# rstd of the first four tiles by ScalarE square root and VectorE reciprocal, bulk loads issued by SyncE, and a reordered prologue

## The chip, the cores and the metric

The kernel runs on 1 core of one Trainium2 chip. Times are device microseconds (us) of one execution; a median of several executions is quoted. Most of the argument is read from traces, where the place of a single instruction is given to 0.01 us. A trace is one execution of each kernel.

Engines in profile lines: PE is TensorE (matmuls), PEld its weight loads, DVE is VectorE, ACT is ScalarE, POOL is GpSimd, SP is SyncE. SPq and ACTq are the queues on which these two issue DMAs.

## The reference, cut to what matters

The input x has 2048 tokens of 448 values. One layer norm feeds two branches, a linear attention with softmax features and a mixer with two MLPs; the output is their sum.

```python
x = A_x
xn = _layernorm(x, axis=-1)          # (x - mean) / sqrt(var + 1e-5)
return x + _A_ref(xn, A_wqkv, A_w_phi, A_wo) + _B_ref(xn, B_w1, B_w2, B_w3, B_w4)
```

Every later step needs xn, and TensorE needs it transposed (features on the partitions).

## The kernel before: the parts that the change and the argument touch

The tokens are 16 tiles of 128. For each tile VectorE takes statistics, GpSimd makes rstd as (var + eps) to the power -0.5, VectorE applies it, TensorE transposes the tile into PSUM, and ScalarE (for tiles 10 and 11 VectorE) copies the transposed tile to xnT in SBUF.

```python
def ln_stats(stt, mvt, src, i):                      # VectorE
    R.ew(dve, "bn_stats", stt[:, i, 0:6], src[:, i, 0:D])
    R.ew(dve, "bn_aggr", mvt[:, i, 0:2], stt[:, i, 0:6])

def ln_scale(mvt, rst, a, n, neg):                   # GpSimd
    R.ew(pool, "tensor_scalar", mvt[:, a:a + n, 2], mvt[:, a:a + n, 1], LN_EPS, 1.0, op0=ALU.add, op1=ALU.mult)
    R.ew(pool, "tensor_tensor", rst[:, a:a + n, 0], mvt[:, a:a + n, 2], mhalf[:, 0:n], op=ALU.pow)
    # [cut]
for i in range(10):
    ln1_stats(i, 1, 0)            # ln_stats, then ln_scale, of tile i
    if i:
        ln1_apply(dve, i - 1)
```

PSUM is used as four pairs of banks, 0 to 3. The program makes two instructions on one pair exclude each other: a matmul that starts a new result waits until the engine that reads the old one is done. The prologue is a list of steps played in order. Each engine keeps the order in which its own instructions were recorded, so the list is also the order of ScalarE's queue. The number after a step such as `(xn_T, 5, 2)` is its PSUM pair; for V, WA and WC it stands in a table.

- `spin`: matmuls without use, which keep TensorE busy while it waits.
- `xn_T, i, b`: transposes of tile i into pair b, then the copy to xnT.
- `V(i, k)`: half k of the value projection of tiles i and i + 1 (8, then 6 matmuls). `v_out` is its copy by ScalarE.
- `WA(g, k)`, `WC(g, k)`: parts of x times w1 for tokens 512 g to 512 g + 511; `wa_out` and `wc_out` are their gelus on ScalarE.
- `FO`: folding w_phi into weights. After the prologue come eight rounds "ps" of k and q projections, then the second MLP in pairs p of w3 columns, halves `a(p)` and `b(p)`, with the up-projection `f` and the attention tiles `N` between.

```python
vps = {i: v_pair(i, b) for i, b in ((0, 2), (2, 3), (4, 3), (6, 1), (8, 1), (10, 1), (14, 3))}
wcs = {g: wc_pair(g, b) for g, b in ((0, 2), (1, 3), (2, 0), (3, 3))}
spin(19, 256)
play([(xn_T, 0, 0), (spin, 3, 256), (xn_T, 1, 1), (spin, 4, 256), V(0, 0), (xn_T, 2, 0), V(0, 1), (xn_T, 3, 1),
      (spin, 2, 256), V(2, 0), (v_out, 0, 2), WA(0, 0), (xn_T, 4, 1), (xn_T, 5, 2), V(2, 1), (v_out, 2, 3),
      WA(0, 1), (xn_t, 6, 1, 0), WC(0, 0), (xn_t, 7, 1, 1), (xn_e, 6, 1, 2), WC(0, 1), (wa_out, 0, 0), (wc_out, 0, 2),
      # [cut: V(4), V(6)]
      WA(1, 0), (xn_T, 8, 2, 2), WC(1, 0), WA(1, 1), (xn_T, 10, 1, 2, "DVE"), (ln1_end,), WC(1, 1), (wc_out, 1, 3),
      (wa_out, 1, 0), V(8, 0), FO(1, 0, 0), V(8, 1), (v_out, 8, 1),
      # [cut]
```

The softmax here doesn't subtract the row's maximum and nothing guards it: scores larger than these inputs give would overflow.

## Time and profile before

Median 176.25 us (176.02 to 176.55, 3 runs).

| what | before | where it is read |
|---|---|---|
| PE busy | 168.9 of 174.0 us, 97% | page, part 1 |
| chain that ended last | PE for 94% | page, part 4 |
| first real transposes / of tile 3 | 5.70 / 9.30 us | timeline |
| V(8,0) starts | 20.70 us | timeline |
| break before V(8,0) | 19.86 to 20.70 us | chain in order of time |
| round ps 0 | 31.52 to 37.21 us | timeline |

These are lines of the page of the kernel before: busy time by engine, and the chain of work that ended last.

```profile
PE 168.9 (97%) x2254; PEld 90.4 (52%) x2254; DVE 114.2 (66%) x258; ACT 81.9 (47%) x94; POOL 92.3 (53%) x131
PE 94%; DVE 3%; issue 1%; POOL 0%; ACT 0%; DVEq 0%
```

TensorE is the limit for nearly all of the span. A change of the prologue can win where TensorE waits, at the start and in the break before V(8,0), and where matmuls are stretched without idle time in the records, as in round ps 0 (see the prediction).

This is the timeline of the kernel before at the start. The columns are start in us, duration in us, engine, line, operation, output<-input and count; in square brackets is the idle time before it and who ended it.

```profile
3.41 0.63 DVE L212 BATCH_NORM_STATS2 st<-xtok 128x6 f32<-128x448 bf16 x1
4.35 0.19 POOL L212 TENSOR_SCALAR mv<-mv 128x1 f32<-128x1 f32 x1 [1.69 <-DVE mv L212]
4.62 0.57 POOL L212 TENSOR_TENSOR rs<-mv,mhalf 128x1 f32<-128x1 f32 x1
5.23 0.41 DVE L212 TENSOR_SCALAR xn<-xtok,mv,rs 128x512 bf16<-128x512 bf16 x1 [0.25 <-POOL rs L212]
6.31 0.38 DVE L212 TENSOR_SCALAR xn<-xtok,mv,rs 128x512 bf16<-128x512 bf16 x1
...
7.41 0.41 DVE L212 TENSOR_SCALAR xn<-xtok,mv,rs 128x512 bf16<-128x512 bf16 x1
...
8.54 0.41 DVE L212 TENSOR_SCALAR xn<-xtok,mv,rs 128x512 bf16<-128x512 bf16 x1
```

The two GpSimd steps of tile 0 take 0.84 us from 4.35 to 5.19, in which VectorE does the statistics of tile 1. Tiles 0 to 3 are applied at 5.23, 6.31, 7.41 and 8.54.

And this is the timeline of the kernel before at the break.

```profile
19.45 0.40 PE L204 MATMUL bank<-ident,xn 64*128 64x64 bf16 x16
19.68 0.49 PE L200 MATMUL bank<-xnT,w 64*128 64x256 bf16 x6
19.88 0.76 DVE L212 COPY xnT<-bank 128x512 bf16<-128x512 bf16 x2 [0.34 <-PE bank L204]
20.70 0.93 PE L200 MATMUL bank<-wv,xnT 64*128 64x448 bf16 x8 [0.53 <-DVE xnT L212]
```

V(8,0), the last line, has its tiles but not its pair: VectorE is still copying tiles 10 and 11 out of it. The idle time in brackets counts from the modelled end of the last matmul; the chain counts 0.84 us from the last issue.

### The profile page before, as it was taken

The numbers are of one execution on the slowest core, as the hardware profiler recorded it, in microseconds if no ns is written. First come the engines' busy times: TensorE is split into PE (matmuls) and PEld (weight loads), VectorE is DVE, ScalarE is ACT, GpSimd is POOL, SyncE is SP. The second block draws the span as 40 slices with busy tenths as digits, with TensorE's granted clock in tenths as the row PEclk, the third lists the DMA queues.
The fourth block names the chain that finished last, engine by engine and source line by source line (L and its number), as shares of the span: only waits on it lengthen the run. The fifth ranks groups of instructions, "written<-read, shape, count | busy, mean of one in ns | idle before, by whom it ended". The sixth has DMA issues, their size and how long they took to land.

```text
span 174.0 us, 5178 instructions
## 1 busy us (share of the span) xinstructions
PE 168.9 (97%) x2254; PEld 90.4 (52%) x2254; DVE 114.2 (66%) x258; ACT 81.9 (47%) x94; POOL 92.3 (53%) x131
## 2 busy tenths in 40 slices
PE   7899899999999999999999999999999999999993
PEld 5466577454555554554544555545545555545451
DVE  4999876185999999985687962445417424474711
ACT  2269866779877777956225322224214222224000
POOL 3786470007779999940549389440721714523740
PEclk9999999999999999999999999999999999999999
DMA  5994532115991102034012732034411220314331
GB/s 159 326 263 79 134 73 50 31 39 148 399 348 41 30 17 47 4 34 90 10 24 60 79 77 59 28 87 95 90 30 53 60 57 4 85 30 34 83 105 30
DMA packets 32678, 15.20 MB, mean 87 GB/s; under 512 B 24080, under 2 KB 32016, under 8 KB 32656
## 3 DMA queue, kind: packets, MB, share of 16 engines
q1 hardware_dynamic: 29888, 12.96, 31.8%
q10 hardware_dynamic: 2768, 1.92, 3.5%
q8 instruction: 17, 0.28, 0.7%
q14 instruction: 5, 0.04, 0.1%
HBM read 7.14 MB, written 1.84 MB: 52 GB/s over the span
## 4 chain that ended last, share of the span: by engine, by line
PE 94%; DVE 3%; issue 1%; POOL 0%; ACT 0%; DVEq 0%
PE bank L200 92%; PE bank L204 1%; DVE vaug L212 1%; DVE st L212 1%; DVE xnT L212 0%; DVE xn L212 0%; ACT xnT L208 0%; POOL rs L212 0%; DVE mv L212 0%; DVEq L173 0%; DVE gT L212 0%; POOL mv L212 0%
## 5 line engine op out<-in xcount | busy, mean ns | idle before, releaser
L208 ACT ACTIVATE phik<-bank 128x1024 bf16<-128x1024 f32 (+1 forms) x44 | 42.3, 984 | 60.2 <-PE bank L200 60.2
L200 PE MATMUL bank<-gT,w 64*128 64x512 bf16 x392 | 50.0, 377 | 0.0
L212 DVE TENSOR_TENSOR vaug<-bank,vaug 128x464 f32<-128x464 f32 (+3 forms) x65 | 32.6, 512 | 23.0 <-PE bank L200 21.4
L200 PE MATMUL bank<-w,phik 64*128 64x448 bf16 (+1 forms) x420 | 45.0, 349 | 0.0
L212 POOL TENSOR_TENSOR xnT<-vaug 128x196 bf16<-128x196 f32 (+1 forms) x32 | 18.1, 587 | 46.3 <-DVE vaug L212 46.3
L200 PEld LDWEIGHTS bank<-w,phik 64*128 64x128 bf16 (+1 forms) x420 | 21.7, 94 | 21.2 <-issue 0.4
L212 POOL TENSOR_TENSOR phik<-phik,rks 128x1792 bf16<-128x1792 bf16 x8 | 25.6, 3214 | 10.6 <-DVE rks L212 10.5
L200 PEld LDWEIGHTS bank<-gT,w 64*128 64x128 bf16 x392 | 17.5, 94 | 17.5 <-ACT phik L208 0.4
L212 POOL TENSOR_TENSOR vaug<-xn,xtok 128x448 f32<-128x448 bf16 x16 | 16.2, 1033 | 0.2 <-DVE vaug L212 0.2
L212 DVE TENSOR_REDUCE ksum<-phik 128x64 f32<-128x1792 bf16 x8 | 16.1, 2010 | 0.0
L212 DVE RECIPROCAL vaug<-bank 128x16 f32<-128x16 f32 x16 | 4.1, 257 | 17.9 <-PE bank L200 17.9
L200 PE MATMUL bank<-xnT,wpq 64*128 64x512 bf16 x112 | 14.7, 376 | 0.0
L200 PE MATMUL bank<-wv,xnT 64*128 64x448 bf16 x112 | 13.5, 351 | 0.6 <-DVE xnT L212 0.5
L212 POOL TENSOR_TENSOR rs<-mv,mhalf 128x1 f32<-128x1 f32 (+2 forms) x20 | 13.0, 651 | 1.7
L200 PE MATMUL bank<-wo,xnT 64*128 64x448 bf16 (+1 forms) x106 | 13.4, 349 | 0.0
L200 PE MATMUL bank<-xnT,w 64*128 64x512 bf16 (+2 forms) x168 | 13.3, 306 | 0.0
L200 PE MATMUL bank<-w,hT 64*128 64x448 bf16 x112 | 13.2, 349 | 0.0
L200 PE MATMUL bank<-wpk,xnT 64*128 64x448 bf16 x112 | 13.2, 349 | 0.0
L212 DVE TENSOR_TENSOR xn<-bank,xn 128x512 bf16<-128x512 f32 (+1 forms) x16 | 9.2, 620 | 3.1 <-PE bank L200 3.1
L212 DVE BATCH_NORM_STATS2 st<-xtok 128x6 f32<-128x448 bf16 x16 | 9.9, 617 | 0.0
L208 ACT ACTIVATE xnT<-bank 128x512 bf16<-128x512 bf16 x12 | 6.7, 595 | 5.7 <-PE bank L204 5.5
L212 POOL TENSOR_SCALAR g_tok<-xn,rs 128x512 bf16<-128x512 bf16 x12 | 9.1, 771 | 0.3
(64 smaller groups left out, 169.4 us busy)
## 6 DMA issues: line engine op xcount, KB each, us to landing
w<-in_B_w_dram SPq DMA_DIRECT2D x2, 896.0 KB, 5.8
out_dram<-vaug SPq DMA_DIRECT2D x15, 112.0 KB, 1.9
w<-in_B_w_dram SPq DMA_DIRECT2D x1, 1568.0 KB, 11.6
xtok<-in_A_x_dram ACTq DMA_DIRECT2D x2, 448.0 KB, 7.6
xtok<-in_A_x_dram SPq DMA_DIRECT2D x2, 224.0 KB, 5.9
w<-in_B_w_dram ACTq DMA_DIRECT2D x2, 224.0 KB, 6.1
wo<-in_A_wo_dram SPq DMA_DIRECT2D x2, 224.0 KB, 6.7
w<-in_B_w_dram SPq DMA_DIRECT2D x1, 336.0 KB, 3.5
```

The source lines that it names most:

```text
L200: self.op("PE", lambda e: e.matmul(out, lhsT, rhs, start=start, stop=stop, skip_group_check=True), [out], [lhsT, rhs], tile=self._tile(lhsT))
L204: self.op("PE", lambda e: e.transpose(out, in_, ident), [out], [in_, ident], tile=self._tile(in_))
L208: self.op("ACT", lambda e: e.activation(out, in_, func, **kw), [out], [in_] + aps)
L212: self.op(eng, lambda e: getattr(e, name)(out, *args, **kw), [out], aps)
```

## The change

Its intent: tiles 0 to 3 should reach TensorE earlier by replacing the GpSimd power with a square root on ScalarE and a reciprocal on VectorE. ScalarE must then be free early, so SyncE issues the bulk loads. Later tiles come a little later, and the order and pairs of the prologue are set to that; tiles 10 and 11 get another pair. Gelu now needs a second table load. Round ps 0 is reordered. The diff, cut to its core:

```diff
+        load_lap(w1, B_w1)                       # all on SyncE, after x tiles 4 to 7
+        load_x(8, 4)
+        load_x(12, 4)
+        R.dma(wphi[0:CR, :, :], ...)
-        R.op("ACT", lambda e: e.preload_act_table_set("gelu_apprx_tanh_and_others"), [], [])
-        load_lap(w1, B_w1, ("ACT", "ACT"))
-        load_x(8, 4, "ACT")
-        load_x(12, 4, "ACT")
-        R.dma(wphi[0:CR, :, :], ..., "ACT")
+        tables("sqrt_and_others")
+        R.ew(dve, "memset", epsb[:, :], LN_EPS)
@@
-        for i in range(10):
+        def ln1_two(i):
+            for j in (i, i + 1):
+                ln_stats(st, mv, xtok, j)
+                R.act(rs[:, j, 1:2], mv[:, j, 1:2], ACT.Sqrt, bias=epsb[:, 0:1])
+            for j in (i, i + 1):
+                R.ew(dve, "reciprocal", rs[:, j, 0:1], rs[:, j, 1:2])
+                ln1_apply(dve, j)
+        ln1_two(0)
+        # [cut: spins and the transposes of tiles 0 and 1, as before]
+        ln1_two(2)
+        for i in range(4, 10):
             ln1_stats(i, 1, 0)
-            if i:
+            if i > 4:
                 ln1_apply(dve, i - 1)
@@
-        vps = {... (2, 3), (4, 3), (6, 1), ...}      # and wcs (1, 3)
+        vps = {... (2, 3), (4, 1), (6, 3), ...}      # and wcs (1, 2)
-              (spin, 2, 256), V(2, 0), (v_out, 0, 2), WA(0, 0), (xn_T, 4, 1), (xn_T, 5, 2), V(2, 1), (v_out, 2, 3),
-              WA(0, 1), (xn_t, 6, 1, 0), WC(0, 0), (xn_t, 7, 1, 1), (xn_e, 6, 1, 2), WC(0, 1), (wa_out, 0, 0), (wc_out, 0, 2),
+              (spin, 2, 256), V(2, 0), (v_out, 0, 2), (tables, "gelu_apprx_tanh_and_others"), WA(0, 0), (xn_T, 4, 1),
+              V(2, 1), (v_out, 2, 3), (xn_T, 5, 2), WA(0, 1), WC(0, 0), (xn_T, 6, 3), WC(0, 1), (wc_out, 0, 2),
@@   # further on
-              WA(1, 0), (xn_T, 8, 2, 2), WC(1, 0), WA(1, 1), (xn_T, 10, 1, 2, "DVE"), ...
+              ..., WC(1, 1), (xn_T, 8, 1, 2), (wc_out, 1, 2), WA(1, 1), (wa_out, 1, 0), (xn_T, 10, 3, 2, "DVE"), ...
@@   # round ps 0
+            if not ps:
+                play([(k[0],), (q[0],), (k[1],), (k_exp, 0, 1, 0), (k_exp, 0, 1, 1), (w[0],), (q[1],), (q_exp, 0, 0, 0),
+                      (q_exp, 0, 0, 1), V(14, 0), (w[1],), (v_out, 12, 2, "DVE"), V(14, 1), (v_out, 14, 3), (k_norm, 0)])
+                continue
```

More of the change, by code (lines that the diff above doesn't have):

```diff
@@ L306, in bass_parallel_sum__linear_kernel_hedgehog__mixer_s_mlp__prompt_kernel @@
         mhalf = new("mhalf", 8, F32)
+        epsb = new("epsb", 8, F32)
         h3T = view(phik_r, 2 * FC * 512).rearrange("p (b c f) -> p b c f", b=2, c=FC)
@@ L360, in bass_parallel_sum__linear_kernel_hedgehog__mixer_s_mlp__prompt_kernel @@
         load_x(6, 2)
+        load_lap(w1, B_w1)
+        load_x(8, 4)
+        load_x(12, 4)
+        R.dma(wphi[0:CR, :, :], A_w_phi.rearrange("(c q) e f -> (q e) c f", q=4))
         def load_wT(t):
@@ L378, in bass_parallel_sum__linear_kernel_hedgehog__mixer_s_mlp__prompt_kernel, with tables @@
         vp = vaug.rearrange("p t (h e) -> p (t h) e", e=HP)
-        R.op("ACT", lambda e: e.preload_act_table_set("gelu_apprx_tanh_and_others"), [], [])
-        load_lap(w1, B_w1, ("ACT", "ACT"))
-        load_x(8, 4, "ACT")
-        load_x(12, 4, "ACT")
-        R.dma(wphi[0:CR, :, :], A_w_phi.rearrange("(c q) e f -> (q e) c f", q=4), "ACT")
+        def tables(name):
+            R.op("ACT", lambda e: e.preload_act_table_set(name), [], [])
+        tables("sqrt_and_others")
         R.ew(pool, "memset", ident[:, :], 0.0)
@@ L778, in play @@
                 f[0](*f[1:])
-        for i in range(10):
+        def ln1_two(i):
[6 more added lines that the diff above has]
+        ln1_two(0)
+        spin(19, 256)
+        play([(xn_T, 0, 0), (spin, 3, 256), (xn_T, 1, 1)])
+        ln1_two(2)
+        for i in range(4, 10):
             ln1_stats(i, 1, 0)
-            if i:
+            if i > 4:
                 ln1_apply(dve, i - 1)
@@ L799, in ln1_end @@
             late_3()
-        vps = {i: v_pair(i, b) for i, b in ((0, 2), (2, 3), (4, 3), (6, 1), (8, 1), (10, 1), (14, 3))}
+        vps = {i: v_pair(i, b) for i, b in ((0, 2), (2, 3), (4, 1), (6, 3), (8, 1), (10, 1), (14, 3))}
         was = {g: wa_pair(g, b) for g, b in ((0, 0), (1, 0), (2, 0), (3, 2))}
-        wcs = {g: wc_pair(g, b) for g, b in ((0, 2), (1, 3), (2, 0), (3, 3))}
+        wcs = {g: wc_pair(g, b) for g, b in ((0, 2), (1, 2), (2, 0), (3, 3))}
         wds = {h: wd_pair(h, b) for h, b in ((0, 1), (1, 0))}
@@ L820, in FO @@
             return (fps[t, m][k],)
-        spin(19, 256)
-        play([(xn_T, 0, 0), (spin, 3, 256), (xn_T, 1, 1), (spin, 4, 256), V(0, 0), (xn_T, 2, 0), V(0, 1), (xn_T, 3, 1),
-              (spin, 2, 256), V(2, 0), (v_out, 0, 2), WA(0, 0), (xn_T, 4, 1), (xn_T, 5, 2), V(2, 1), (v_out, 2, 3),
-              WA(0, 1), (xn_t, 6, 1, 0), WC(0, 0), (xn_t, 7, 1, 1), (xn_e, 6, 1, 2), WC(0, 1), (wa_out, 0, 0), (wc_out, 0, 2),
-              V(4, 0), V(6, 0), V(4, 1), (v_out, 4, 3), V(6, 1), (v_out, 6, 1),
-              WA(1, 0), (xn_T, 8, 2, 2), WC(1, 0), WA(1, 1), (xn_T, 10, 1, 2, "DVE"), (ln1_end,), WC(1, 1), (wc_out, 1, 3),
-              (wa_out, 1, 0), V(8, 0), FO(1, 0, 0), V(8, 1), (v_out, 8, 1),
+        play([(spin, 4, 256), V(0, 0), (xn_T, 2, 0), V(0, 1), (xn_T, 3, 1),
+              (spin, 2, 256), V(2, 0), (v_out, 0, 2), (tables, "gelu_apprx_tanh_and_others"), WA(0, 0), (xn_T, 4, 1),
+              V(2, 1), (v_out, 2, 3), (xn_T, 5, 2), WA(0, 1), WC(0, 0), (xn_T, 6, 3), WC(0, 1), (wc_out, 0, 2),
+              V(4, 0), (xn_T, 7, 3), (wa_out, 0, 0), V(4, 1), (v_out, 4, 1), V(6, 0),
+              WC(1, 0), V(6, 1), (v_out, 6, 3), WA(1, 0), WC(1, 1), (xn_T, 8, 1, 2), (wc_out, 1, 2), WA(1, 1), (wa_out, 1, 0),
+              (xn_T, 10, 3, 2, "DVE"), (ln1_end,), V(8, 0), FO(1, 0, 0), V(8, 1), (v_out, 8, 1),
               WA(2, 0), FO(1, 0, 1), FO(1, 2, 0), WA(2, 1), (wa_out, 2, 0), FO(1, 2, 1),
@@ L860, in bass_parallel_sum__linear_kernel_hedgehog__mixer_s_mlp__prompt_kernel @@
             w[1]()
-            if ps:
-                w2_out(side[ps], 2)
-            else:
-                v_out(12, 2, "DVE")
-                vps[14][0]()
+            w2_out(side[ps], 2)
             q[1]()
@@ L868, in bass_parallel_sum__linear_kernel_hedgehog__mixer_s_mlp__prompt_kernel @@
                 q_exp(2 * ps, 0, s)
-            if not ps:
-                vps[14][1]()
-                v_out(14, 3)
             if ps in (3, 5):
```

## The prediction

> **What bounds the kernel now.** TensorE: the page has PE busy 168.9 of 174.0 us (97%), and the chain of waits is PE for 94%. From the second operand of V(2,0) at 10.27 us to 171.27 the chain has one break: 19.86 to 20.70, where V(8,0) waits for a VectorE copy (2 x 0.38 us) of tiles 10 and 11, because that copy holds the PSUM pair which V(8,0) needs. So the change can only win in the first 10 us, in that break, and in hidden stalls. Round ps 0 (31.52 to 37.21) takes 5.69 us; its 56 matmuls at their steady spacing (about 0.094 us for 448 columns, 0.107 for 512) are about 5.4. At most 0.3 us is there.
>
> **First 10 us (timeline).** Before: bn_stats 0 at 3.41, GpSimd add and pow (0.19 + 0.57 us) from 4.35 to 5.19, apply 0 at 5.23, apply 1 at 6.31, applies 2 and 3 at 7.41 and 8.54, xnT copies on ScalarE at 6.26, 7.08, 8.82, 9.62.
> After: the pair's two statistics run first (to about 4.98), so apply 0 stays at about 5.1 to 5.2. The square root takes about 0.2 us (estimate: ScalarE copies of 512 and 896 columns take 0.60 and 0.91, so 0.19 is fixed), the reciprocal 0.16 (estimate: 0.257 for 16 elements, 0.55 for 64). Apply 1 moves to about 5.7 (0.6 earlier), but applies 2 and 3 wait for both statistics of their pair: about 7.7 and 8.3. Tile 2 comes later, tile 3 slightly earlier. V(2,0) can then go at about 9.9 instead of 10.27: 0.3 to 0.4 us won, not the 0.6 of apply 1. The new epsb memset may cost 0.1 in front of bn_stats 0. Loads issued by SyncE free ScalarE, whose issues ran to 6.21, just before its first copy; they gate little.
>
> **What it adds.** A second table load, in ScalarE's idle time of 1.19 us between 11.03 and 12.22. The Trainium skill ("ScalarE: Activation LUTs", What ACT_TABLE_LOAD costs) gives about 1283 ns plus 1380 ns drain; the trace agrees with the first (1.28 us at 2.26 and at 32.92) and shows no drain (the work before ended at 32.90, the next began at 34.22). So 1.28, nearly hidden.
> The new order puts v_out(2) (0.9 us) before the copy of tile 5 (0.57), whose pair WC(0,0) needs. From the end of V(2,1) that is 0.25 + 0.9 + 0.57 = 1.75 us, against 0.8 of PE work between: a new stall of about 0.9 us near 13.5, before WC(0,0). Tile 4's statistics also start about 0.5 to 1 us later, which the order allows for. In exchange xn_T(10) goes to another pair, and the 0.84 us break before V(8,0) shrinks to 0 to 0.3.
>
> **Sum.** Start -0.35, break -0.65, WC(0,0) +0.9, small pair waits before V(6,0) and xn_T +0.2, ps 0 -0.1: about 0. V(8,0) should start at 20.4 to 21.4 (before 20.70), and all after it is the same PE-bound stream. The order was evidently set by hand for this, so my range leans to a gain.
>
> Predicted 176.1 us, range 175.1 to 177.0. Chance of faster by over 2% 0.02, within 2% 0.96, slower by over 2% 0.02.
>
> **Would show it right or wrong.** Timeline: four Sqrt of about 0.2 us, apply 0 unmoved, apply 1 near 5.7, applies 2 and 3 near 7.7 and 8.3; a 1.28 us table load near 11; waits of PE: a new one of about 0.9 us on a ScalarE xnT copy before WC(0,0), the one on the VectorE copy gone. From V(8,0) to the end the same length within 0.3 us.
>
> **What would make it wrong.** The weights or later x landing late from one queue; a drain around the table load; the first tiles arriving later; a stall in ps 0 that the records hide.

## The result, and the profile after

The changed kernel takes 176.34 us (175.99 to 176.41, 4 runs), the one before 176.13 (175.94 to 176.55, 4 runs). The ratio is 1.0004, with a 95% interval of 0.9981 to 1.0028: no difference that these runs resolve. Ratios here are the mean time of one kernel's fast runs over that of the other's of the same rounds, so not quite the ratio of the medians quoted.

The timeline of the changed kernel at the start:

```profile
4.19 0.29 ACT L208 ACTIVATE rs<-mv,epsb 128x1 f32<-128x1 f32 x1 [0.65 <-DVE mv L212]
4.80 0.13 DVE L212 RECIPROCAL rs<-rs 128x1 f32<-128x1 f32 x1
4.97 0.41 DVE L212 TENSOR_SCALAR xn<-xtok,mv,rs 128x512 bf16<-128x512 bf16 x1
5.49 0.41 DVE L212 TENSOR_SCALAR xn<-xtok,mv,rs 128x512 bf16<-128x512 bf16 x1
...
6.94 0.63 DVE L212 BATCH_NORM_STATS2 st<-xtok 128x6 f32<-128x448 bf16 x1 [0.28 <-DMA xtok<-in_A_x_dram]
...
7.87 0.41 DVE L212 TENSOR_SCALAR xn<-xtok,mv,rs 128x512 bf16<-128x512 bf16 x1
8.39 0.41 DVE L212 TENSOR_SCALAR xn<-xtok,mv,rs 128x512 bf16<-128x512 bf16 x1
```

Tile 1 is applied 0.82 us earlier than before, tile 2 0.46 us later, tile 3 0.15 us earlier. In this execution VectorE also waited for tile 3 to arrive from memory. V(2,0) could go on with tile 3 at 10.00 us instead of 10.27.

The timeline of the changed kernel between 10 and 22 us:

```profile
10.77 1.28 ACT L386 ACT_TABLE_LOAD   x1
12.07 0.60 ACT L208 ACTIVATE xnT<-bank 128x512 bf16<-128x512 bf16 x1
12.56 0.91 ACT L208 ACTIVATE vaug<-bank 128x896 bf16<-128x896 f32 x1
13.36 0.60 ACT L208 ACTIVATE xnT<-bank 128x512 bf16<-128x512 bf16 x1
14.02 0.61 PE L200 MATMUL bank<-xnT,w 64*128 64x256 bf16 x8 [0.78 <-ACT xnT L208]
...
20.16 1.09 ACT L208 ACTIVATE xnT<-bank 128x512 bf16<-128x512 bf16 x2 [0.51 <-PE bank L204]
21.30 0.93 PE L200 MATMUL bank<-wv,xnT 64*128 64x448 bf16 x8 [0.30 <-ACT xnT L208]
```

After the table load ScalarE copies tile 4 (12.07), evicts V(2) (12.56) and only then copies tile 5 (13.36). WC(0,0), at 14.02, needs the pair of tile 5 and waits 0.78 us. In the kernel before, both copies (the first line) went ahead of that eviction:

```profile
12.22 1.09 ACT L208 ACTIVATE xnT<-bank 128x512 bf16<-128x512 bf16 x2 [1.19 <-PE bank L204]
13.19 0.92 ACT L208 ACTIVATE vaug<-bank 128x896 bf16<-128x896 f32 x1
```

Before V(8,0) the wait on the VectorE copy is gone, but there is one on the ScalarE copies of tiles 8 and 9, and V(8,0) starts 0.60 us later than before.

PE's waits in the kernel before, in total (the 1.3 us is the start of the program):

```profile
PE bank L200 <- DVE gT L212: 1.3, 1, 1.3
PE bank L200 <- DVE xnT L212: 0.5, 1, 0.5
PE bank L204 <- DVE xn L212: 0.4, 2, 0.2
```

PE's waits in the changed kernel:

```profile
PE bank L200 <- DVE gT L212: 1.3, 1, 1.3
PE bank L200 <- ACT xnT L208: 1.1, 2, 0.8
PE bank L204 <- DVE xn L212: 0.3, 1, 0.3
```

The 0.5 us on a VectorE copy was exchanged for 1.1 us on ScalarE copies. To compare all kernels I cut TensorE's time by five marks: the first transpose of tile 3, V(8,0), the starts of rounds ps 0 and ps 1, and the last group of matmuls. The columns "tile 3" and "last" give the marks themselves, the others the lengths between marks in each kernel's trace.

| kernel | tile 3 | tile 3 to V(8,0) | V(8,0) to ps 0 | ps 0 | ps 1 to last | last |
|---|---|---|---|---|---|---|
| before | 9.30 | 11.40 | 10.82 | 5.69 | 133.12 | 170.33 |
| changed | 9.03 | 12.27 | 10.83 | 5.48 | 133.41 | 171.02 |
| difference | -0.27 | +0.87 | +0.01 | -0.21 | +0.29 | +0.69 |

The start won 0.27 us and ps 0 another 0.21; the way from tile 3 to V(8,0) lost 0.87. The +0.29 in the last part, where no instruction was changed, was not expected. The traces differ by more than the medians do, and that last part is one reason, as will be seen.

### The profile page after: what moved, and what is told of

It is laid out like the page before. It is cut to its first block, busy times and chain, and to the rows that moved or that the text cites. A ratio compares the mean times of both kernels' runs of the same rounds, so it can differ in the third digit from the quotient of the medians.

```text
span 174.7 us, 5180 instructions
## 1 busy us (share of the span) xinstructions
PE 169.2 (97%) x2254; PEld 90.8 (52%) x2254; DVE 114.5 (66%) x263; ACT 84.3 (48%) x99; POOL 88.7 (51%) x123
## 4 chain that ended last, share of the span: by engine, by line
PE 90%; ACT 3%; DMA 3%; DVE 1%; ACTq 0%; issue 0%; DVEq 0%
PE bank L200 90%; DMA xtok<-in_A_x_dram 3%; ACT xnT L208 2%; ACT vaug L208 1%; ACT L386 1%; PE bank L204 1%; ACTq L218 0%; DVE st L212 0%; DVE xn L212 0%; DVE vaug L212 0%; DVEq L173 0%; DVE mv L212 0%; DVE rs L212 0%
## 5 line engine op out<-in xcount | busy, mean ns | idle before, releaser
L212 POOL TENSOR_TENSOR rs<-mv,mhalf 128x1 f32<-128x1 f32 (+2 forms) x16 | 10.8, 675 | 1.3
L212 POOL TENSOR_SCALAR mv<-mv 128x1 f32<-128x1 f32 (+2 forms) x16 | 3.8, 238 | 12.5 <-DVE mv L212 12.0
L200 PEld LDWEIGHTS bank<-xnT,w 64*128 64x128 bf16 (+1 forms) x168 | 6.9, 98 | 4.6 <-ACT xnT L208 1.3
```

The source lines that it names most:

```text
L200: self.op("PE", lambda e: e.matmul(out, lhsT, rhs, start=start, stop=stop, skip_group_check=True), [out], [lhsT, rhs], tile=self._tile(lhsT))
L212: self.op(eng, lambda e: getattr(e, name)(out, *args, **kw), [out], aps)
```

## The experiments

The theory: what the square root wins at the start is lost again by the new order, because WC(0,0) waits for the copy of tile 5 queued behind v_out(2). The rivals: the second table load is what costs (PE's chain of waits does run through it), or the moved loads, or ScalarE as such is the limit, so that a wait removed comes back elsewhere.

### 1. One part at a time

`loads_only`: the kernel before, with the bulk loads moved to SyncE.

```diff
+        load_lap(w1, B_w1); load_x(8, 4); load_x(12, 4); R.dma(wphi...)      # SyncE
-        load_lap(w1, B_w1, ("ACT", "ACT")); load_x(8, 4, "ACT"); load_x(12, 4, "ACT"); R.dma(wphi..., "ACT")
```

> The kernel before, with only the bulk loads (w1, x tiles 8 to 15, w_phi) moved from ScalarE's queue to SyncE's. Theory (the loads gate little): ScalarE's first copy starts at most 0.2 us earlier than 6.26, V(2,0) and V(8,0) stay within 0.2 us of 10.27 and 20.70, and the time is the same within 0.2%. Rival (freeing ScalarE and the queue order are what pays or costs): V(8,0) moves by 0.4 us or more. The landing of x tile 3 is to be read too: 4.3 us from its issue before, 5.2 in the changed kernel; if the queue order does that, this run shows it as well.

Measured: ratio 0.9999 (0.9981 to 1.0018). ScalarE's first copy moved from 6.26 to 6.00, and V(8,0) stayed at exactly 20.70. The rival falls. This agrees with the Trainium skill, "DMA: Bandwidth & Descriptors", Issuing engines are not separate DMA queues: DMAs of different issuers share the same 16 engines, and another issuer only saves sequencer time. x tile 3 landed 4.8 us after its issue. Over all traces with the order of loads unchanged up to x tile 3, it landed after 4.3 to 5.2 us with the bulk loads on SyncE (six traces) and after 4.3 to 5.3 with them on ScalarE (seven). So the 5.2 of the changed kernel's trace is scatter of that landing, not shown to be an effect of the queue.

`sqrt_old_order`: the changed kernel with the prologue list, pairs and round ps 0 of before.

```diff
-        vps, wcs, play(...) and round ps 0 of the changed kernel
+        vps, wcs, play(...) and round ps 0 of before, with the second table load after v_out(0)
```

> The changed kernel with the prologue order, the PSUM pairs and round ps 0 of before: square root, reciprocal and loads alone. Theory: the start gains 0.3 us (V(2,0) at about 10.0), the transposes of tile 5 and of tile 7 wait for VectorE's later applies (0.4 to 0.5 and about 0.2 us), the 0.84 us break before V(8,0) is there, and V(8,0) starts at 20.9 to 21.4; no wait on a ScalarE copy before WC(0,0) as large as 0.78. Rival (the new order rescues nothing, the loss is that of the statistics path alone): V(8,0) as late as 21.3 or later with the same 0.78 wait.

Measured: 1.0026 (0.9995 to 1.0057). The start was worth more than I had expected: tile 3 landed in time, its transposes began at 8.63, 0.67 us earlier than before. From there to V(8,0) it took 12.04, which puts V(8,0) at 20.67, below my 20.9 to 21.4. Transposes of tiles 4 and 5 were stretched (0.84 us against 0.49 before), those of tile 7 waited 0.20 us for VectorE, and the break before V(8,0) was there. These two are in PE's timeline:

```profile
11.05 0.84 PE L204 MATMUL bank<-ident,xn 64*128 64x64 bf16 x16
13.86 0.29 PE L204 MATMUL bank<-ident,xn 64*128 64x64 bf16 x8 [0.20 <-DVE xn L212]
```

So late tiles in the old order cost 0.64 us, which cancels the 0.67 won. The new order, with 12.27, does not rescue this; it is 0.2 us worse.

`order_only`: the converse, the kernel before with the new list, pairs and ps 0.

```diff
-        vps, wcs, play(...) and round ps 0 of before
+        vps, wcs, play(...) and round ps 0 of the changed kernel, without the second table load
```

> The kernel before (GpSimd power, ScalarE loads, one table load) with the new prologue order, pairs and round ps 0. Theory: the wait of about 0.8 us before WC(0,0) on the copy of tile 5 comes from the order alone, so it is here too (0.7 to 0.9), V(8,0) starts within 0.3 us of the changed kernel's 21.30 and round ps 0 takes 5.5 us instead of 5.7. Rival (the wait comes from the table load or from the later tiles): it shrinks below 0.4 us and V(8,0) starts at 20.6 or earlier.

Measured: 1.0040 (1.0020 to 1.0059), slower by 0.4%. In its timeline WC(0,0) waits as in the changed kernel:

```profile
13.67 0.59 ACT L208 ACTIVATE xnT<-bank 128x512 bf16<-128x512 bf16 x1
14.32 0.28 PE L200 MATMUL bank<-xnT,w 64*128 64x256 bf16 x2 [0.73 <-ACT xnT L208]
```

V(8,0) starts at 21.61, 0.31 us later than in the changed kernel. The way from tile 3 to V(8,0) is 12.25, the same within 0.02 as there, without its square root and without a second table load. The wait belongs to the order. Round ps 0 takes 5.48 here too, so its reordering is worth 0.21 us in either kernel.

`no_second_load`: a wrong result (the relative error was 9), to take away the second table load and nothing else.

```diff
-        tables("sqrt_and_others")                 # and Sqrt
+        tables("gelu_apprx_tanh_and_others")      # and Identity, no load later
-              (v_out, 0, 2), (tables, "gelu_apprx_tanh_and_others"), WA(0, 0), ...
+              (v_out, 0, 2), WA(0, 0), ...
```

> A wrong result on purpose: the changed kernel with Identity in place of Sqrt and the gelu table loaded once at the start, so that the second table load goes away and nothing else. Theory (hidden: the copy of tile 4 and v_out(2) wait for PE anyway): the copy of tile 4 starts about 0.3 us earlier, v_out(2) at most 0.15 us earlier, V(8,0) and the time change by 0.2 us at most. Rival (as the chain of waits has it, which runs through the table load for its whole 1.28 us): V(8,0) starts 0.8 us earlier or more.

Its timeline of ScalarE and PE:

```profile
11.61 0.60 ACT L208 ACTIVATE xnT<-bank 128x512 bf16<-128x512 bf16 x1 [1.19 <-PE bank L204]
12.18 0.92 ACT L208 ACTIVATE vaug<-bank 128x896 bf16<-128x896 f32 x1
12.99 0.59 ACT L208 ACTIVATE xnT<-bank 128x512 bf16<-128x512 bf16 x1
13.64 0.28 PE L200 MATMUL bank<-xnT,w 64*128 64x256 bf16 x2 [0.73 <-ACT xnT L208]
```

V(8,0) came 0.38 us earlier than in the changed kernel, more than the 0.2 allowed, but tile 3's transposes also began 0.34 us earlier, because tile 3 landed in time. From tile 3 to V(8,0) it is 12.23 against 12.27. So the second load costs about 0.04 us in the changed kernel. In its place ScalarE simply idles 1.19 us (first line), and the wait before WC(0,0) is still there. The chain of waits had shown the load for its whole 1.28 us only because it was later than the work it ran beside by a few hundredths: a step on the chain is not worth its length if another chain ends just behind it.

### 2. Mending the order, and a wait found at 82 us

`c5_first`: the copy of tile 5 ahead of v_out(2), and pairs 1 and 3 exchanged for what follows so that tile 6 finds a free pair.

```diff
-              V(2, 1), (v_out, 2, 3), (xn_T, 5, 2), WA(0, 1), WC(0, 0), (xn_T, 6, 3), WC(0, 1), ...
+              V(2, 1), (xn_T, 5, 2), (v_out, 2, 3), WA(0, 1), WC(0, 0), (xn_T, 6, 1), WC(0, 1), ...
               # and pairs 1 and 3 exchanged in V(4), V(6), V(8), V(10), xn_T 7 to 14, FO(1,0), FO(0,2), WD(0)
```

> The changed kernel with the copy of tile 5 queued on ScalarE ahead of v_out(2), and PSUM pairs 1 and 3 exchanged for what follows, so that tile 6 goes to a pair that is free. Theory (the loss is the wait of WC(0,0) for the tile 5 copy behind v_out(2)): the 0.78 us wait before WC(0,0) shrinks to 0.2 or less, the way from the transposes of tile 3 to V(8,0), 12.27 us in the changed kernel and 11.40 in the one before, becomes 11.0 to 11.3, and V(8,0) starts at 20.0 to 20.4. Rival (ScalarE is the limit there, so a wait taken away at one place comes back at the next): the way stays at 11.8 or longer, with new waits on ScalarE copies near V(4,0) or V(8,0).

Measured: ratio 0.9962 (0.9947 to 0.9977), 175.37 us. The wait before WC(0,0) is no longer among PE's waits; V(8,0) starts at 20.21:

```profile
20.21 0.93 PE L200 MATMUL bank<-wv,xnT 64*128 64x448 bf16 x8 [0.30 <-ACT xnT L208]
```

From tile 3 to V(8,0) it takes 11.54, a little more than the 11.0 to 11.3 expected, since the wait on the copies of tiles 8 and 9 stayed (0.30, as in the changed kernel). It did not grow, so the rival, that a removed wait comes back, falls. In the changed kernel the order, and not the square root, was the loss.

The trace of sqrt_old_order had named a wait that no change touches. This is a line of its PE waits:

```profile
PE bank L200 <- DMA gT<-g_tok: 0.6, 1, 0.6
```

At 82 us, half a(7) is the first to read the transposed tiles 4 to 7 of the second layer norm, which SyncE transposes by DMA just before. In this trace the wait is 0.57 us. Other traces have 0 to 0.3 us too much at the same place, but their records give it as issue time. Two kernels tried to remove it.

`before_gate`: the kernel before, with the up-projection ahead of a(7).

```diff
-            b(6), a(7), f(1, 0), b(7), N(1), ...
+            b(6), f(1, 0), a(7), b(7), N(1), ...
```

> The kernel before with one swap at about 82 us: the first up-projection of the output (28 matmuls) goes ahead of the first half of w3 pair 7, which is the first to read the transposed tiles 4 to 7. Theory: PE waits there for the last DMA transpose, 0 to 0.6 us and different in every execution (0.00, 0.13, 0.24, 0.57 in the traces so far whatever the prologue), and this is most of the scatter of the times; here the wait is gone in the trace, the time is 0.1 to 0.4 us (0.05 to 0.25%) shorter and the runs scatter less. Rival (an artefact of the profile, or paid back later): no change within 0.1%, same scatter.

Measured: ratio 1.0003 (0.9987 to 1.0020), a miss: no gain, and runs from 175.75 to 176.52. From ps 1 to the last group it takes 133.38, more than the 133.12 of before. The wait on the DMA did not appear, but the two halves a(7) and b(7) now stand back to back, and the second's weight loads wait for the first half's matmuls. This is a line of the waits between 80 and 92 us, then one of PE's timeline, both of before_gate:

```profile
PEld bank L200 <- PE bank L200: 0.6, 1, 0.6
```

```profile
85.28 1.92 PE L200 MATMUL bank<-gT,w 64*128 64x512 bf16 x14
```

Elsewhere 14 matmuls of this form (b(p), then a(p + 1), which use another pair of banks) take 1.69 us. So 0.23 us were lost by a new wait.

`before_gate2`: the same with other work between the halves.

```diff
-            b(6), a(7), f(1, 0), b(7), N(1), (w2_norm, 10), A(8, 9, 10, 11),
+            b(6), f(1, 0), a(7), N(1), (w2_norm, 10), A(8, 9, 10, 11), b(7),
```

> The kernel before with the swap at 82 us done without its fault: the up-projection goes ahead of the first half of w3 pair 7, and the attention tile 1 and its statistics go between the two halves, which stood back to back in the first try and lost 0.23 us there on each other. Theory: no wait on the DMA transpose and no stall between the halves; from the start of round ps 1 to the last matmul 133.1 to 133.2 us (133.12 in the trace of before that had no wait, up to 133.88 in others), time 0.1 to 0.3 us below before on average (ratio 0.998 to 0.9995) with less scatter. Rival: paid back later, 133.4 or longer and a ratio of 1.000 or more.

Measured: 0.9981 (0.9965 to 0.9998), and 133.14 from ps 1 to the last group. The interval lies just below 1. The six runs lay between 175.74 and 176.37, the eleven of before between 175.84 and 176.85; that less scatter is due to this is plausible but not tested further. From ps 1 to the last group the traces without either swap have 133.12, 133.18, 133.20, 133.20, 133.28, 133.41, 133.42 and 133.88 us; those with the mended swap 133.14, 133.19 and 133.19.

`before_pairs_gate`: no square root. The break before V(8,0) is removed by pairs alone, with the new ps 0 and the first, faulty swap.

```diff
-  V(8) and V(10) in pair 1, FO(1,0) in 3, WC(1) in 3, (xn_T, 8, 2, 2), (xn_T, 14, 3, 2), FO(0,2) in 3, WD(0) in 1
+  V(8) and V(10) in pair 3, FO(1,0) in 1, WC(1) in 2, (xn_T, 8, 3, 2), (xn_T, 14, 1, 2), FO(0,2) in 1, WD(0) in 3
```

> The kernel before, statistics, loads and prologue order kept, with other PSUM pairs for tiles 8 and 10 (so that V(8,0) waits for no VectorE copy), round ps 0 as in the changed kernel, and the swap at 82 us. Theory: V(8,0) starts at 19.8 to 20.0 instead of 20.70, round ps 0 takes 5.5 us instead of 5.7, no wait at 82: together 1.0 to 1.4 us, ratio 0.992 to 0.995. Rival (the break before V(8,0) hid other lateness, of tiles 12 to 15 or of ScalarE): waits appear between 20 and 31 us and the gain is below 0.5 us.

Measured: 0.9966 (0.9952 to 0.9979), 175.33 us. V(8,0) starts at 19.92, 10.71 after tile 3, and ps 0 takes 5.48, as expected. From V(8,0) to ps 0 it takes 11.03 instead of 10.82, because WA(2,0) now waits for a gelu, and 133.43 after ps 1 shows the faulty swap. These two explain the ratio, less good than 0.992 to 0.995.

`c5_x3_gate`: c5_first, the faulty swap, and x tile 3 loaded ahead of half of wv.

```diff
-        load_lap(wv, A_wqkv[:, 896:1344], ("ACT", "SP"))
         load_x(3, 1, "ACT")
+        load_lap(wv, A_wqkv[:, 896:1344], ("ACT", "SP"))
```

> c5_first plus x tile 3 issued ahead of the first half of wv on ScalarE's queue, plus the swap at 82 us: the square root path with both of the order's losses mended. Theory: tile 3 lands by 5.5 us, VectorE does not wait for it, the transposes of tile 3 start at 8.5 to 8.8, V(8,0) at 19.6 to 20.0, ratio to the kernel before 0.991 to 0.995, and at most 0.3 us better than the version without the square root. Rival (wv late instead): V(0,0) starts later than 7.0 or is stretched by 0.3 us or more.

Measured: 0.9984 (0.9971 to 0.9998), 175.82 us, a miss. Tile 3 did land after 2.7 us and VectorE did not wait, but the transposes of tile 3 began at 9.16. By its wording the rival, a late wv, is met: V(0,0) starts at 7.57, after 7.0. But wv's first half landed at about 7.05 (issued at 1.75, 5.3 us), and TensorE was still on its spins until V(0,0). In c5_first V(0,0) starts at 6.89, so a late wv can account for at most about 0.16 of the 0.68 us. These are the three spins between the transposes of tiles 0 and 1, the transposes of tile 1, and the four spins before V(0,0), in PE's timeline of c5_x3_gate:

```profile
5.75 0.82 PE L200 MATMUL bank<-gT 128*128 128x256 bf16 x3
6.51 0.40 PE L204 MATMUL bank<-ident,xn 64*128 64x64 bf16 x8
6.83 0.80 PE L200 MATMUL bank<-gT 128*128 128x256 bf16 x4
```

And the same in c5_first:

```profile
5.69 0.50 PE L200 MATMUL bank<-gT 128*128 128x256 bf16 x3
6.12 0.29 PE L204 MATMUL bank<-ident,xn 64*128 64x64 bf16 x8
6.34 0.61 PE L200 MATMUL bank<-gT 128*128 128x256 bf16 x4
```

The same spins take 1.3 to 1.6 times as long. The Trainium skill, "TensorE: Matmul & The Clock Gate", Part 1, says why this can be: TensorE runs at half its clock until it has been busy for a window of about 3.4 us, the window is free-running, and so the point of change is different in each run. The traces agree: the change comes before 5.7 us in c5_first and near 7 us in c5_x3_gate. It is read from the durations alone; the granted clock in the records is 1.00 in both. In the fourteen traces these three spins take 0.50 us in ten, 0.66 to 0.68 in two (best_a, before_gate) and 0.82 in two (loads_only and this one). The spins fit a tile 1 that arrives at 6.7 us (before); with the square root it is ready at 5.85, and slow spins stand in its way. Since only one trace of each kernel was taken, how often this happens in one kernel is open.

### 3. The best of both ways, and why the loads moved

`best_b`: without the square root. before_pairs_gate with the mended swap and `FO(1, 0, 1)` ahead of `WA(2, 0)`.

> Without the square root: the kernel before with free PSUM pairs for tiles 8 and 10, round ps 0 as in the changed kernel, one fold half ahead of the third w1 group, and the mended swap at 82 us. Theory: V(8,0) at 19.8 to 20.0, 10.8 us from there to round ps 0, 5.48 us in it, 133.1 to 133.2 after it: last matmul near 169.35 (170.33 before), ratio 0.992 to 0.9945. Rival: a new wait eats the 0.2 us of the fold half.

`best_a`: with the square root. c5_first with the mended swap and the edit below. The fold half was moved as in best_b as well, which the expectation does not mention.

```diff
-              ..., WA(1, 0), WC(1, 1), (xn_T, 8, 3, 2), (wc_out, 1, 2), ...
+              ..., WA(1, 0), (xn_T, 8, 3, 2), WC(1, 1), (wc_out, 1, 2), ...
```

> With the square root: c5_first with the transposes of tiles 8 and 9 ahead of the second half of WC(1), and the mended swap at 82 us. Theory (from tile 4 on VectorE's pace sets when tiles 8 to 11 are ready, in both ways of the first tiles, so that the earlier start is worth nothing): V(8,0) at 19.8 to 20.1 and the time within 0.15% of best_b. Rival (the earlier start counts once the order fits): V(8,0) at 19.5 or earlier and the time 0.2% below best_b or more.

Measured: best_b 0.9938 (0.9919 to 0.9956), 175.13 us; best_a 0.9928 (0.9913 to 0.9942), 174.97 us. Both are correct and beat both kernels; they differ by 0.1%, which is not resolved. This is the whole list of PE's waits in best_a:

```profile
PE bank L200 <- DVE gT L212: 1.3, 1, 1.3
```

V(8,0) starts at 20.23 in best_b and 20.16 in best_a, both a little later than expected, in best_b because tile 3's transposes began only at 9.52. The theory gave the right number, but no wait shows its reason: in best_a TensorE does not wait for VectorE's tiles between tile 3 and V(8,0). It is close, though: tiles 10 and 11 are applied by 19.43, 0.15 us before their weight loads begin (19.58), so a way shorter by more than that would meet this limit next. TensorE starts 0.57 us earlier than in best_b (transposes of tile 3 at 8.95), and takes 11.21 us from there to V(8,0), against 10.71 in best_b. Of these 0.5 us, about 0.3 is before WC(0,0), where the copies of tiles 4 and 5 follow the table load and end at about 13.15. These are the two copies, the end of the transposes of tile 5 and the weight load of WC(0,0) in the timeline of best_a:

```profile
11.99 1.16 ACT L208 ACTIVATE xnT<-bank 128x512 bf16<-128x512 bf16 x2
12.27 0.25 PE L204 MATMUL bank<-ident,xn 64*128 64x64 bf16 x3
13.20 0.11 PEld L200 LDWEIGHTS bank<-xnT,w 64*128 64x128 bf16 x4 [0.53 <-ACT xnT L208]
```

The load is not what holds WC(0,0) up. The copy of tile 5 takes about 0.60 us, so it began at about 12.55, when the transposes of tile 5 ended (12.52), while the load (10.70 to 11.98) delayed only the copy of tile 4. What is late is tile 5, transposed behind V(2,1) in this order and ahead of it in that of before. It could not have come much earlier: VectorE had applied it by 11.86, and its weight loads begin at 11.96. So VectorE's pace does stand behind this loss, through an order that is fitted to it. All this is read from the timeline; a run without the load was not made.

`sqrt_scalar_loads`: the changed kernel with the bulk loads left on ScalarE.

```diff
-        load_lap(w1, B_w1); load_x(8, 4); load_x(12, 4); R.dma(wphi...)      # SyncE
+        load_lap(w1, B_w1, ("ACT", "ACT")); load_x(8, 4, "ACT"); load_x(12, 4, "ACT"); R.dma(wphi..., "ACT")
```

> The changed kernel with the bulk loads left on ScalarE's queue. Theory (the loads had to move for the square root, not for their own sake): ScalarE issues until 6.2 us, so the first square root runs at 6.2 or later instead of 4.19, the transposes of tile 0 start at 7.4 or later instead of 5.44, and the time is 1.0 to 2.0 us longer than the changed kernel's. Rival (issues and square roots go side by side): within 0.3 us of it.

Measured: 1.008 (1.0036 to 1.0123). One of its four runs was slow and is left out of the ratio; another, at 178.95 us and a clock of 0.99, is in it and lifts it. The trace is the better measure. The first two square roots run at 5.56, not after 6.2, since ScalarE finished its issues sooner than before (5.51). The transposes of tile 0 start at 6.56 instead of 5.44, those of tile 3 at 9.77 instead of 9.03, and V(8,0) at 22.04 instead of 21.30. The direction holds, at 0.74 us instead of 1.0 to 2.0. The loads had to move for the square root, and by themselves they were worth nothing.

## Why the prediction was right, point by point

- **Time.** 176.1 predicted, range 175.1 to 177.0; 176.34 measured. The forecast "within 2%" held. The lean to a gain, put in because the order had evidently been set by hand, had no ground in the sum, and no gain was measured.
- **The limit.** Right: TensorE, with gains only at the start, in the break, and a little in ps 0.
- **Start.** Predicted 0.3 to 0.4 us, with V(2,0) at about 9.9: measured 0.27, at 10.00. The estimates of applies 0 to 3 (5.1 to 5.2, 5.7, 7.7, 8.3) compare with 4.97, 5.49, 7.87 and 8.39. In this execution x tile 3 came late: its statistics begin at 6.94, against 6.53 in sqrt_old_order, where it landed in time and the start won 0.67. So the applies came earlier than estimated (4.93, 5.45, 7.42 and 7.94 there), and a late DMA, which the prediction named only as a risk, took 0.4 us of that back. That 0.3 to 0.4 lies near 0.27 is luck. The square root took 0.29 us, not 0.19: the estimate came from copies without a bias operand. The Trainium skill, "ScalarE: Activation LUTs", What ACT_TABLE_LOAD costs, has the number: about 280 ns plus 0.833 ns per column when the bias is a per-partition operand.
- **Second table load.** "Nearly hidden": shown by no_second_load, 0.04 us.
- **WC(0,0).** Predicted about 0.9 us near 13.5: measured 0.78 us before 14.02, and shown by order_only and c5_first to come from the order of ScalarE's queue.
- **The break.** Predicted to shrink from 0.84 to 0 to 0.3. It is 0.30 by the idle view. From the last issue of the transposes of tiles 10 and 11 (about 20.86) to V(8,0) it is 0.44, on the count by which it was 0.84. So 0.40 was won, not 0.65.
- **Small pair waits.** The whole way from tile 3 to V(8,0) was put at +0.45 (-0.65 + 0.9 + 0.2) and measured +0.87. This is the term of the sum that was off most: with 0.78 at WC(0,0) and -0.40 at the break, 0.49 is left for the small waits put at 0.2. Taken away one at a time, the way is 12.27 in the changed kernel, 11.54 without the wait of WC(0,0) (c5_first) and 11.21 without that before V(8,0) as well (best_a). The last 0.5 against best_b (10.71) is located only in part.
- **ps 0.** Predicted 0.1, at most 0.3; measured 0.21, in every kernel with that order.
- **V(8,0).** Predicted 20.4 to 21.4, measured 21.30.
- **The rest the same within 0.3.** From V(8,0) to the last group: 149.72 against 149.63. The agreement is partly luck: 0.21 won in ps 0 and 0.29 lost at 82 us, at a wait that varies between executions. The prediction did not see that wait at all.

## What to carry to other kernels

An earlier first result is worth only what the queue behind it lets through: here 0.3 to 0.7 us at the start were lost again, mainly because one copy, whose PSUM pair TensorE needed next, stood behind another in ScalarE's queue. When an order is changed, go through each pair of banks and ask which engine frees it and what stands ahead of that in its queue. And take a change apart in both directions (the new order without the new arithmetic, and the reverse) before judging either: the useful parts of this one, the pair of tiles 10 and 11 and round ps 0, have nothing to do with the square root.

## What the Trainium skill lacked or had wrong

- "ScalarE: Activation LUTs", What ACT_TABLE_LOAD costs, gives a drain of about 1380 ns beside 1283 ns of load. Here a load takes 1.28 us and no drain is seen: in the changed kernel v_out(0) ended at 10.75, the load ran from 10.77 to 12.05, and the next copy began at 12.07.
- "DMA: Bandwidth & Descriptors", DMA Transpose (X-bar), has no durations; elsewhere the page has a bandwidth for one kernel and a decode cost of small tiles, but no time to landing. Here one transpose of a 128x512 tile took SyncE 1.19 to 2.52 us to issue and landed 2.4 to 4.4 us after its issue, in kernels with the same instructions there; in sqrt_old_order, where one landed after 4.3 us, TensorE waited 0.57 us for it.
- The same page gives a fixed cost, said to be smaller when memory is less loaded, and a bandwidth, but not the scatter of one load in one place. One 112 KB load among others at the start landed after 4.3 to 5.3 us, and moved the start of the kernel by up to 0.4 us.
- "TensorE: Matmul & The Clock Gate", Part 1, puts the start of the fast clock at about 4 us into the activity, within 500 ns from run to run. Here, with the first spin at 1.25 us, one spin already took 0.27 us at 4.79 in c5_first (0.42 at 5.07 in before), while in c5_x3_gate the transposes at 6.51 still took 0.40 us instead of 0.29. So it came at most 3.6 us after the first spin in one, and over 5.2 us after it in the other. The page calls the cost under 1% of a span, which the about 0.5 us of c5_x3_gate against c5_first fits; what it lacks is that matmuls without use can hold up real work behind them while they run slowly.
- "TensorEngine Tiling (Array Packing)", Gotcha 1: PSUM Pressure, says that different row tiles cannot use the same PSUM bank at one time, but not what it costs. The two halves of a pair here use the same two banks with the row tiles exchanged. Back to back they lost 0.23 us (14 matmuls in 1.92 us instead of 1.69), and it went away when other work was put between them. That the shared banks are the cause was not tested apart.
